# Constant-operand matmuls in the filler bank where a planned kernel leaves TensorE without work

## The chip, the cores and the metric

The program runs on one core of a Trainium2 chip. The metric is the device time of one execution in microseconds (us). The engines' names are those of the profile: PE is TensorE's matmul side and PEld its weight loads, ACT is ScalarE, DVE is VectorE, POOL is GpSimd, SP is SyncE, whose queue issues most DMAs.

## The reference

Four layers run one after the other over an activation `x` of 2048 tokens by 1024 features, each with a residual: A, B, A, B. Both kinds have 32 heads of 32 features. Kind A is linear attention with softmax feature maps, kind B is full softmax attention without a mask:

```python
def _A_ref(x, wqkv, w_phi, wo):
    ...
    phi_q = jnp.concatenate([_softmax(pq, axis=-1), _softmax(-pq, axis=-1)], axis=-1)
    phi_k = jnp.concatenate([_softmax(pk, axis=-1), _softmax(-pk, axis=-1)], axis=-1)
    kv = jnp.einsum("bhsf,bhsd->bhfd", phi_k, v)
    ...
def _B_ref(x, wqkv, wo):
    ...
    scores = jnp.einsum("bhqd,bhkd->bhqk", q, k) * (Dh ** -0.5)
    p = _softmax(scores, axis=-1)
    o = jnp.einsum("bhqk,bhkd->bhqd", p, v)
    ...
x = x + _A_ref(_layernorm(x, axis=-1), A_wqkv, A_w_phi, A_wo)
x = x + _B_ref(_layernorm(x, axis=-1), B_wqkv, B_wo)
x = x + _A_ref(_layernorm(x, axis=-1), A_wqkv, A_w_phi, A_wo)
x = x + _B_ref(_layernorm(x, axis=-1), B_wqkv, B_wo)
```

In each B layer 32 heads x 2048 x 2048 scores, 134 million, go through an exponential.

## The kernel before, in words

The activation lives in SBUF transposed, in `xT`: 8 slabs of 128 features by 2048 tokens. The tokens are worked on in four chunks of 512. The program is written as a list of operations (`Op`: an engine, a modelled duration, what it depends on, the buffers that it holds and a priority). `Sched.run` is a planner in Python that plays this list through once, before anything is built: each modelled engine takes, when it is free, the ready operation of lowest priority number whose buffers can be had. The order that comes out is the order in which the instructions are then written, so on the chip every engine follows a fixed list. The planner's clock is a model and never changes speed (`MM` = 0.2165 us for a 512-column matmul).

PSUM has eight banks of 512 columns. In a B layer's attention they are shared out: banks 0 to 2 and 3 to 5 are two score buffers (class `S`), bank 6 collects one output (class `acc`), and bank 7 is the filler bank (`FIL`, class `fil`).

Attention goes in steps, which are called steps here throughout. A step covers three units; a unit is one head, one chunk of 512 queries and one block of 128 keys. In a step:
- three score matmuls of 32 rows each fill three banks (line 886, in `attention`); they lie beside each other in TensorE's rows;
- one ACTIVATE takes the exponential of all three banks, 128 x 1536 (line 892). A later step may write those banks once it is done;
- six matmuls of 32 columns each add V and the sum of the exponentials to bank 6 (line 920). They are issued four together, beside each other in TensorE's columns.

A B layer has 4096 units, so 1366 steps in both. Query chunks 0 and 1 are done first, head group by head group, then chunk 2 and then chunk 3 for all groups.

All other matmuls that fall into attention are fillers: the keys, values and queries of later head groups (`b_k`, `b_v`, `b_q`, `q_away`), the output projections of finished query chunks (`b_o`, in the last layer `b_last`, line 847), and in the first B layer the next A layer's keys. Each filler is a group of eight matmuls of 128 x 512 in four operations, accumulating in bank 7, which is held from the group's first matmul until its result has been read out. Fillers take the bank strictly in the order of their priorities. A projection group needs the eight head groups' outputs `oT[0]` to `oT[7]`, and each of its four operations waits for two of them alone.

The names that matter below: line 886 is the score matmul, line 892 the exponential, line 920 the V and sum matmul, line 847 a filler of the last projection, `onesD` a constant 128 x 128 matrix, `Sched.live` the count of buffers in use by class, `bank_used` the state of the eight banks.

Of the kernel before, what the change touches and what calls it, by code (L numbers as in the profile page):

```python
# [18 lines left out]
C512 = 512  # L19
# [3 lines left out]
class Buf:  # L23
# [4 lines left out]
    def __init__(self, kind, size, cls, banks=None):  # L28
        self.kind, self.size, self.cls, self.banks = kind, size, cls, banks
        self.left, self.at, self.with_ = 0, None, ()  # L30
# [11 lines left out]
LAT = {"PE": 0.25, "ACT": 0.2, "DVE": 0.1, "POOL": 0.2, "SP": 2.0, "AQ": 2.0}  # L42
# [3 lines left out]
class Sched:  # L46
    def __init__(self, sbuf_bytes, quota):
        self.ops = []
        self.quota = quota
        self.live = {}  # L50
        self.free = [(0, sbuf_bytes)]
        self.bank_used = [False] * 8
        self.peak = 0
        self.total = sbuf_bytes
        self.queue = {}

    def op(self, eng, dur, fn, deps=(), bufs=(), prio=0.0, lat=None, mode=None):
        o = Op(eng, dur, LAT[eng] if lat is None else lat, fn, tuple(bufs), prio, mode, len(self.ops))
        for d in deps:
            if d is not None:  # L60
                d.out.append(o)
                o.ndep += 1
        for b in o.bufs:
            b.left += 1
        self.ops.append(o)
        return o
# [75 lines left out]
    def run(self):  # L142
        engines = list(LAT)
        ready = {e: [] for e in engines}
        busy = {e: 0.0 for e in engines}
        mode = {e: None for e in engines}
        events = []
        n = 0

        first = {}  # L150
        for o in self.ops:
            for b in o.bufs:
                k = (o.prio, o.seq)
                for x in (b, *b.with_):
                    if id(x) not in first or k < first[id(x)][0]:
                        first[id(x)] = (k, x)
        for k, b in sorted(first.values(), key=lambda f: f[0]):
            self.queue.setdefault(b.cls, [[], 0])[0].append(b)
        todo = sorted(o.prio for o in self.ops)
        front = 0  # L160
        started = {}
        for o in self.ops:
            if o.ndep == 0:
                heapq.heappush(ready[o.eng], (o.prio, o.seq, o))
        t, left, order = 0.0, len(self.ops), []
        while left:
            moved = False
            for e in engines:
                if busy[e] > t + 1e-9 or not ready[e]:
                    continue  # L170
                skipped = []
                pick = None
                while ready[e] and len(skipped) < 60:
                    item = heapq.heappop(ready[e])
                    if item[0] <= todo[front] + WINDOW and self._alloc(item[2].bufs):
                        pick = item[2]
                        break
                    skipped.append(item)
                for s in skipped:
                    heapq.heappush(ready[e], s)  # L180
                if pick is None:
                    continue
                d = pick.dur
                if pick.mode is not None:
                    if mode[e] is not None and mode[e] != pick.mode:
                        d += SWITCH
                    mode[e] = pick.mode
                pick.start = t
                started[pick.prio] = started.get(pick.prio, 0) + 1
                while front < len(todo) - 1 and started.get(todo[front], 0):  # L190
                    started[todo[front]] -= 1
                    front += 1
                busy[e] = t + d
                order.append(pick)
                left -= 1
                moved = True
                n += 1
                heapq.heappush(events, (t + d, n, pick, True))
                n += 1
                heapq.heappush(events, (t + d + pick.lat, n, pick, False))  # L200
            if moved:
                continue
            if not events:
                stuck = [(o.prio, o.eng, [(b.cls, b.at) for b in o.bufs]) for e in engines for _, _, o in ready[e]][:8]
                raise AssertionError(f"nothing can start at {t:.1f}: {left} left, {stuck}, live {self.live}")
            t = events[0][0]
            while events and events[0][0] <= t + 1e-9:
                _, _, o, own = heapq.heappop(events)
                if not own:
                    for b in o.bufs:  # L210
                        b.left -= 1
                        if b.left == 0:
                            self._release(b)
                for x in o.out:

                    if own != (x.eng == o.eng and x.eng not in ("SP", "AQ")):
                        continue
                    x.ndep -= 1
                    if x.ndep == 0:
                        heapq.heappush(ready[x.eng], (x.prio, x.seq, x))  # L220
        self.end = t
        return order
# [8 lines left out]
         "e": 6, "vp": 6, "e1": 4, "vp1": 4, "E": 5, "q2": 3, "kt": 3, "w2": 8, "w2o": 3, "oT": 26, "T": 4, "den": 2,  # L231
         "lnt": 6, "lnw": 2, "lnw1": 1, "eq": 8, "ns": 4, "cw": 6, "hl": 6, "oc": 2, "slab": 7, "slabk": 3, "fin": 4,
         "rs": 8, "pkf": 1}


def act_us(n):
# [7 lines left out]
MM = 0.2165  # L244
# [3 lines left out]
def kernel(  # L248
# [11 lines left out]
    nc = tc.nc  # L260
    P = nc.NUM_PARTITIONS
    _, S, D = A_x.shape
    PO = D // P
    G = PO
# [20 lines left out]
    onesD = const.tile([P, P], BF16, tag="onesD")  # L285
# [6 lines left out]
    pick = const.tile([P, 4], F32, tag="pick")  # L292
# [30 lines left out]
    xT = const.tile([P, PO, S], BF16, tag="xT")  # L323
    ARENA = SBUF_ARENA
    arena = arena_p.tile([P, ARENA // 2], BF16, tag="arena")
    psum = psum_p.tile([P, 8 * C512], F32, tag="psum")
# [10 lines left out]
    sch = Sched(ARENA, QUOTA)  # L337
# [31 lines left out]
    TAIL = [(x,) for x in (7, 0, 1, 2, 3, 4, 5)]  # L369
# [96 lines left out]
    def slab(cls, prio, src, n, deps=(), q="SP"):  # L466
        b, v = sb(cls, PO, n)
        o = dma(prio, lambda: (nc.sync if q == "SP" else nc.scalar).dma_start(out=v(), in_=src),
                deps, [b], q=q, kb=2 * n)
        return b, v, [o] * 4  # L470
# [352 lines left out]
    def b_o(ft, c, prio, w, oT, banks, after=None):  # L823
        wb, ww, wd = w
        pb, pv = ps("fil", banks)
        m = mmg2(pb, pv, lambda po: ww()[:, po, :], lambda po: oT[po][1](),
                 [[oT[2 * i][2], oT[2 * i + 1][2], after] for i in range(4)], wd,
                 [wb] + [oT[i][0] for i in range(G)], prio)
        return op("DVE", dve_us(512), lambda: nc.vector.tensor_tensor(
            out=xT[:, ft, csl(c)], in0=xT[:, ft, csl(c)], in1=pv(), op=ALU.add), [m], [pb], prio)  # L830
# [148 lines left out]
    for layer in range(2):  # L979
# [73 lines left out]
        oTs, last_s = attention(at, kT, vT, q_of, gate)  # L1053
        if last:
            bo_s = [slab("slab", at + 160 + fc, B_o[:, :, fc * C512:(fc + 1) * C512], C512) for fc in range(2)]
        for qc, p0, gap, banks in ((0, 163, 1.5, FIL), (1, 176, 1.5, FIL), (2, 251, 1.5, FIL), (3, 340, 1, TAIL)):
            after = last_s if banks is TAIL else None
            if last:
                gap = {0: 6, 1: 6, 2: 9, 3: 1}[qc]
                p0 = {0: 163, 1: 200, 2: 251, 3: 340}[qc]  # L1060
                for t in range(TB):
                    for fc in range(2):
                        b_last(qc, t, fc, at + p0 + gap * (2 * t + fc), bo_s[fc], oTs[qc], banks,
                               ("ACT", "DVE")[fc] if banks is TAIL else "DVE", after)
            else:
                adds = []
                for ft in range(G):
                    w = slab("w2o", at + p0 + gap * ft - 6, B_o[:, :, ft * P:(ft + 1) * P], P)
                    adds.append(b_o(ft, qc, at + p0 + gap * ft, w, oTs[qc], banks, after))
                xdone[qc] = adds  # L1070
        if not last:

            kv = new_kv()
            for c, p0 in ((0, 190), (1, 220), (2, 265)):
                xb, xv, fin = xnA[c] = layernorm(c, at + p0, FIL, True)
                w = [(wk_slab(at + p0 + 2 + 14 * fc, fc, "slabk"), wv_slab(at + p0 + 2.5 + 14 * fc, fc, cls="slabk")) for fc in range(2)]
                a_keys(c, at + p0 + 2, [w[0][0], w[1][0]], [w[0][1], w[1][1]], kv, FIL, True, 3.5)
                xnA[c] = dma(at + p0 + 4, lambda c=c, xv=xv: nc.sync.dma_start(
                    out=xd_v[:, c, :, :], in_=xv()), fin, [xb], kb=1024)

    for o in sch.run():
        o.fn()
# [30 lines left out]
```

## Time and profile before

| what | value |
| --- | --- |
| median of 3 runs | 2716.61 us (2715.13 to 2718.79) |
| the profiled execution's own time | 2719.31 us |
| its span, first to last instruction | 2717.5 us |
| PE busy | 2417.6 us (89%) |
| ACT busy | 2194.0 us (81%) |
| DVE busy | 1136.0 us (42%) |
| mean granted TensorE clock | 0.906 |

Busy time of PE is read with care: its matmuls overlap, and a matmul takes twice as long when the granted clock is 0.50 (1.2 GHz) as when it is 1.00 (2.4 GHz). A busy PE at half clock does half the work. A window's clock between the two is the mean of stretches at either level.

### The profile page before, as it was taken

The numbers are of one execution on the slowest core, as the hardware profiler recorded it, in microseconds if no ns is written. First come the engines' busy times: TensorE is split into PE (matmuls) and PEld (weight loads), VectorE is DVE, ScalarE is ACT, GpSimd is POOL, SyncE is SP. The second block draws the span as 40 slices with busy tenths as digits, with TensorE's granted clock in tenths as the row PEclk, the third lists the DMA queues.
The fourth block names the chain that finished last, engine by engine and source line by source line (L and its number), as shares of the span: only waits on it lengthen the run. The fifth ranks groups of instructions, "written<-read, shape, count | busy, mean of one in ns | idle before, by whom it ended". The sixth has DMA issues, their size and how long they took to land.

```text
span 2717.5 us, 42396 instructions
## 1 busy us (share of the span) xinstructions
PE 2417.6 (89%) x17730; PEld 774.3 (28%) x17984; DVE 1136.0 (42%) x1614; ACT 2194.0 (81%) x1919; POOL 25.3 (1%) x72
## 2 busy tenths in 40 slices
PE   5999998999988988989888999999998898888887
PEld 2443332222222222332313333222222122112112
DVE  4996653333322335655516665233333222222112
ACT  5335546999999999999983553899999999999995
POOL 0000000000000000000000000000000000000000
PEclk9999999999997889999969999999998698668657
DMA  7120003111121212224122000311211011001000
GB/s 166 42 65 1 5 4 65 42 32 45 37 57 40 56 39 65 78 71 119 30 64 97 1 6 3 74 36 34 67 34 26 18 38 32 18 16 32 19 12 22
DMA packets 185760, 116.08 MB, mean 43 GB/s; under 512 B 103904, under 2 KB 175584, under 8 KB 184800
## 3 DMA queue, kind: packets, MB, share of 16 engines
q1 hardware_dynamic: 181344, 109.10, 15.3%
q10 hardware_dynamic: 4224, 4.26, 0.6%
q8 instruction: 140, 2.29, 0.4%
q14 instruction: 52, 0.43, 0.1%
HBM read 61.93 MB, written 15.73 MB: 29 GB/s over the span
## 4 chain that ended last, share of the span: by engine, by line
ACT 45%; PE 35%; issue 10%; DVE 7%; DMA 2%; SPq 1%; ACTq 0%; DVEq 0%
ACT arena L892 43%; PE psum L619 16%; PE psum L920 8%; PE psum L886 5%; DVE arena L562 2%; SPq L404 1%; PE psum L714 1%; DVE arena L571 1%; PE psum L383 1%; DVE arena L460 1%; PE psum L847 1%; ACT arena L558 1%; DVE arena L456 1%; DVE arena L608 1%; PE psum L701 1%
## 5 line engine op out<-in xcount | busy, mean ns | idle before, releaser
L892 ACT ACTIVATE arena<-psum 128x1536 bf16<-128x1536 f32 (+1 forms) x1366 | 1859.8, 1505 | 92.8 <-PE psum L886 50.6
L619 PE MATMUL psum<-arena 128*128 128x512 bf16 x3631 | 954.1, 386 | 60.1 <-DVE arena L460 19.9
L920 PE MATMUL psum<-arena 128*32 128x512 bf16 x4096 | 800.7, 436 | 16.1 <-ACT arena L892 10.2
L920 PE MATMUL psum<-arena,ones_bf 128*32 128x512 bf16 x4096 | 801.6, 437 | 0.0
L886 PE MATMUL psum<-arena 32*128 32x512 bf16 x4096 | 590.0, 428 | 162.6 <-ACT arena L892 152.2
L619 PEld LDWEIGHTS <-arena 128*128 128x128 bf16 x3840 | 318.7, 98 | 562.7 <-issue 282.2
L886 PEld LDWEIGHTS <-arena 32*128 32x128 bf16 x4096 | 167.0, 92 | 708.2 <-issue 698.5
L932 DVE COPY arena<-psum 128x512 f32<-128x512 f32 x128 | 88.4, 691 | 599.7 <-PE psum L920 597.3
L920 PEld LDWEIGHTS <-arena 128*32 128x32 bf16 x4096 | 160.5, 96 | 396.8 <-issue 391.0
L943 DVE RECIPROCAL arena<-arena 128x128 f32<-128x128 f32 x256 | 219.1, 912 | 77.3 <-DMA arena<-arena 76.0
L778 DVE CAST arena<-psum 128x512 bf16<-128x512 f32 x116 | 80.1, 690 | 333.4 <-PE psum L619 211.1
L920 PEld LDWEIGHTS <-ones_bf 128*32 128x32 bf16 x4096 | 158.3, 96 | 47.6 <-issue 46.9
L423 ACT ACTIVATE arena<-xT 128x2048 bf16<-128x2048 bf16 x26 | 50.1, 1934 | 105.4 <-DVE xT L754 40.5
L558 ACT ACTIVATE arena<-psum 128x512 bf16<-128x512 f32 x80 | 43.2, 610 | 101.3 <-PE psum L619 68.6
L671 ACT ACTIVATE arena<-psum 128x512 bf16<-128x512 f32 x128 | 70.3, 598 | 43.6 <-PE psum L619 39.2
L456 DVE TENSOR_TENSOR arena<-xT,arena 128x1024 f32<-128x1024 bf16 x64 | 78.0, 1220 | 63.9 <-ACT arena L445 63.4
L947 DVE TENSOR_TENSOR arena<-arena 64x512 bf16<-64x512 f32 x128 | 87.8, 686 | 29.1 <-PE psum L920 20.8
L777 ACT CAST arena<-psum 128x512 bf16<-128x512 f32 x44 | 25.5, 584 | 88.0 <-PE psum L619 66.8
L571 DVE TENSOR_TENSOR arena<-psum,arena 128x1024 bf16<-128x1024 f32 x64 | 78.3, 1224 | 42.8 <-PE psum L619 38.7
L460 DVE TENSOR_TENSOR arena<-arena 128x1024 bf16<-128x1024 f32 x64 | 77.2, 1224 | 21.3 <-ACT arena L450 20.0
L562 DVE TENSOR_REDUCE arena<-arena 128x32 f32<-128x1024 bf16 x64 | 77.7, 1213 | 16.6 <-ACT arena L558 15.5
L718 ACT COPY arena<-psum 128x512 f32<-128x512 f32 x64 | 37.3, 583 | 55.4 <-PE psum L714 46.6
(79 smaller groups left out, 955.2 us busy)
## 6 DMA issues: line engine op xcount, KB each, us to landing
arena<-arena SPq DMA_DIRECT2D x128, 128.0 KB, 2.3
arena<-in_B_wqkv_dram SPq DMA_DIRECT2D x32, 256.0 KB, 4.6
arena<-arena SPq DMA_DIRECT2D x256, 32.0 KB, 1.9
arena<-in_B_wo_dram SPq DMA_DIRECT2D x32, 256.0 KB, 3.2
arena<-wd_k SPq DMA_DIRECT2D x8, 1024.0 KB, 5.8
arena<-in_A_wqkv_dram SPq DMA_DIRECT2D x8, 1024.0 KB, 5.3
arena<-in_A_wqkv_dram ACTq DMA_DIRECT2D x4, 1024.0 KB, 6.1
arena<-in_A_wo_dram SPq DMA_DIRECT2D x4, 1024.0 KB, 7.2
```

Of the source, the lines that this page charges most:

```text
L456: s1 = op("DVE", dve_us(1024), lambda pr=pr, w_v=w_v: nc.vector.tensor_tensor(out=w_v(), in0=xT[:, pr, csl(c)], in1=m_v().unsqueeze(1).to_ ...
L460: fin.append(op("DVE", dve_us(1024), lambda pr=pr, w_v=w_v: nc.vector.tensor_tensor(out=xv()[:, pr, :], in0=w_v(), in1=r_v().unsqueeze(1). ...
L562: red = op("DVE", dve_us(1024), lambda ev=ev, sv=sv: nc.vector.reduce_sum(out=sv(), in_=ev().rearrange("p s (h d) -> p (s h) d", d=DH), ax ...
L571: ml = op("DVE", dve_us(1024), lambda vpv=vpv, wv_=wv_, sv=sv: nc.vector.tensor_tensor(out=wv_()[:, :, :, 0:DH], in0=vpv().rearrange("p (h ...
L619: nc.tensor.matmul(pv(), lhsT=lhs(po), rhs=rhs(po), start=(po == 0), stop=(po == PO - 1))
L778: return op("DVE", dve_us(512), lambda: nc.vector.tensor_copy(out=dst(), in_=src()), [dep], bufs, prio)
L886: nc.tensor.matmul(out=s_v()[:, x * C512:(x + 1) * C512], lhsT=kT[g][1]()[r, pp, d * P:(d + 1) * P], rhs=q_of[(qc, g)][1]()[r, (pp + j // ...
L892: ex = op("ACT", act_us(w * C512), lambda s_v=s_v, e_v=e_v, w=w: nc.scalar.activation(out=e_v()[:, 0:w * C512], in_=s_v(), func=ACT.Exp), ...
L920: nc.tensor.matmul(out=a_v()[col:col + 32, :], lhsT=v_v()[:, kc % 4, o:o + DH] if what == 0 else ones_bf[:], rhs=ev()[:, x * C512:(x + 1) ...
L932: cp = op("DVE", dve_us(512), lambda t_v=t_v, a_v=a_v: nc.vector.tensor_copy(out=t_v(), in_=a_v()), [last], [a_b, t_b], prio - 4)
L943: rc = [op("DVE", 128 * 8 / 960 + 0.12, lambda b=b, d_v=d_v, r_v=r_v: nc.vector.reciprocal(out=r_v()[:, b * P:(b + 1) * P], in_=d_v()[:, b ...
L947: s = [op("DVE", dve_us(512), lambda a=a, b=b, k=k, o_v=o_v, r_v=r_v, T=T: nc.vector.tensor_tensor(out=o_v()[a, :], in0=T[k][1]()[a, :], i ...
```

## The change

Three things are added. The planner gets an operation `idle`: one 128 x 512 matmul of `onesD` by the first chunk of `xT`, written to bank 7, whose result nobody reads. When the modelled TensorE is free, nothing that is ready can start, a score buffer is live, the modelled TensorE has worked less than 75% (`KEEP`) of the last 3.4 us (`SPELL`), no filler is live and bank 7 is free, an `idle` is placed. Last, the projections of chunks 0 to 2 wait with their first matmul until the last head group's output is there; before, they had no such wait.

```diff
+                if pick is None and e == "PE" and self.idle is not None and self.live.get("S", 0):
+
+                    recent = [r for r in recent if r[1] > t - SPELL]
+                    worked = sum(r[1] - max(r[0], t - SPELL) for r in recent)
+                    if worked < KEEP * SPELL and not self.live.get("fil", 0) and not self.bank_used[7]:
+                        pick = Op("PE", MM, LAT["PE"], self.idle, (Buf("ps", 0, "idle", [(7,)]),), 0.0, "n", 0)
+                        pick.bufs[0].left = 1
+                        self.queue["idle"] = [list(pick.bufs), 0]
+                        assert self._alloc(pick.bufs)
+                        left += 1
                 if pick is None:
                     continue
+                if e == "PE":
+                    recent.append((t, t + pick.dur))
...
-                started[pick.prio] = started.get(pick.prio, 0) + 1
+                if pick.fn is not self.idle:
+                    started[pick.prio] = started.get(pick.prio, 0) + 1
...
+SPELL = 3.4
+KEEP = 0.75
...
-            after = last_s if banks is TAIL else None
+            after = [last_s] if banks is TAIL else oTs[qc][G - 1][2]
...
+    def idle():
+        nc.tensor.matmul(psum[:, 7 * C512:8 * C512], lhsT=onesD[:], rhs=xT[:, 0, 0:C512], start=True, stop=True)
+    sch.idle = idle
```

The built program has 562 such matmuls, line 1099, each with a weight load. Counted from the order by steps (0 to 682 in the first B layer, 683 to 1365 in the second): 63 in steps 287 to 328, 20 in 405 to 416, 7 in 573 to 576, 62 in 641 to 681, 5 at the second layer's start, 63 in 970 to 1011, 159 in 1098 to 1203, 176 in 1247 to 1364, and 7 alone. In steps 264 to 277 and 947 to 960 there is neither a filler nor an `idle`. Other lines of the kernel move by 17: line 886 becomes 903, line 920 becomes 937, line 847 becomes 864.

First place: PE late in the second B layer's attention, just ahead of the scores of step 1262, before. `arena` and `psum` are the work areas in SBUF and PSUM, and a wait on Activation is a wait for ScalarE.

```order
L920 LDWEIGHTS arena
L920 MATMUL psum<-arena 32x512
L920 LDWEIGHTS ones_bf
L920 MATMUL psum<-arena,ones_bf 32x512
L886 LDWEIGHTS arena
L886 MATMUL psum<-arena 128x512 [waits Activation_49]
```

The same place on PE now:

```order
L937 LDWEIGHTS arena
L937 MATMUL psum<-arena 32x512
L937 LDWEIGHTS ones_bf
L937 MATMUL psum<-arena,ones_bf 32x512
L1099 LDWEIGHTS onesD
L1099 MATMUL psum<-xT,onesD 128x512
L903 LDWEIGHTS arena
L903 MATMUL psum<-arena 128x512 [waits Activation_49]
```

Between the V and sum matmuls and the next scores, which wait for an exponential, there is now one `idle`, which waits for nothing.

Second place: PE in the second B layer, just ahead of the scores of step 1120, before. Line 847 is an operation of the projection of query chunk 2.

```order
L920 LDWEIGHTS ones_bf
L920 MATMUL psum<-arena,ones_bf 32x512
L847 LDWEIGHTS arena
L847 MATMUL psum<-arena 128x512
L847 LDWEIGHTS arena [waits DVE_49]
L847 MATMUL psum<-arena 128x512
L886 LDWEIGHTS arena
L886 MATMUL psum<-arena 128x512 [waits Activation_49]
```

The same place on PE now:

```order
L937 LDWEIGHTS ones_bf
L937 MATMUL psum<-arena,ones_bf 32x512
L1099 LDWEIGHTS onesD
L1099 MATMUL psum<-xT,onesD 128x512
L903 LDWEIGHTS arena
L903 MATMUL psum<-arena 128x512 [waits Activation_49]
```

Before, the group's eight matmuls stood two by two in steps 1089, 1119, 1162 and 1204, and held bank 7 all that while; now they stand together in steps 1204 to 1207, and steps 1098 to 1203 hold `idle` matmuls.

## Rows read from the trace of the kernel before

**Rows 1.** The page: busy tenths in 40 slices, and the granted clock.

```profile
PE   5999998999988988989888999999998898888887
ACT  5335546999999999999983553899999999999995
PEclk9999999999997889999969999999998698668657
```

**Rows 2.** Waits: engine, line and what it waited for; total us, times, longest.

```profile
PE psum L886 <- ACT arena L892: 152.2, 326, 1.5
...
ACT arena L892 <- PE psum L886: 50.6, 59, 2.3
...
ACT arena L892 <- PE psum L920: 38.3, 95, 0.5
```

**Rows 3.** Line 892 alone by stretch: length, ACT busy and count, clock, DMA.

```profile
1944.50:2078.90 134.40, 134.28 (x100) 1.00 0.18 48
904.80:920.40 15.60, 15.60 (x12) 1.00 0.32 77
448.30:499.60 51.30, 48.40 (x37) 1.00 0.17 41
831.10:892.70 61.60, 57.35 (x42) 0.68 0.09 22
998.40:1017.40 19.00, 16.16 (x12) 0.68 0.07 18
1360.60:1420.30 59.70, 55.98 (x41) 0.65 0.25 71
2109.70:2172.00 62.30, 57.73 (x42) 0.66 0.08 20
2290.00:2449.40 159.40, 146.25 (x106) 0.63 0.07 17
2509.10:2688.20 179.10, 163.09 (x118) 0.60 0.05 13
2597.60:2658.80 61.20, 54.67 (x40) 0.50 0.03 7
...
2082.00:2100.00 18.00, 15.19 (x11) 0.53 0.05 13
```

**Rows 4.** All engines by stretch: PE, PEld, DVE, ACT, POOL busy (count), clock.

```profile
1944.50:2078.90 134.40, 125.23 (x1066) 35.18 (x1084) 45.24 (x61) 134.28 (x100) 0.00 (x0) 1.00 0.18 48
920.70:936.90 16.20, 14.25 (x126) 4.16 (x128) 6.40 (x8) 16.10 (x14) 0.00 (x0) 1.00 0.38 89
2290.00:2449.40 159.40, 130.76 (x956) 29.82 (x956) 30.72 (x40) 146.25 (x106) 0.00 (x0) 0.63 0.07 17
2597.60:2658.80 61.20, 53.59 (x353) 11.05 (x350) 9.46 (x14) 54.67 (x40) 0.00 (x0) 0.50 0.03 7
998.40:1017.40 19.00, 13.84 (x112) 3.46 (x109) 9.28 (x11) 17.30 (x14) 0.00 (x0) 0.68 0.07 18
```

**Rows 5.** PE in order of time, half clock, no filler: start, length, what.

```profile
2625.95 0.61 PE L886 MATMUL psum<-arena 32*128 32x512 bf16 x3 [0.64 <-ACT arena L892]
...
2627.46 0.61 PE L886 MATMUL psum<-arena 32*128 32x512 bf16 x3
...
2629.15 0.61 PE L886 MATMUL psum<-arena 32*128 32x512 bf16 x3 [0.53 <-ACT arena L892]
```

**Rows 6.** ACT in order of time, the same stretch.

```profile
2627.64 2.79 ACT L892 ACTIVATE arena<-psum 128x1536 bf16<-128x1536 f32 x2 [0.41 <-PE psum L920]
2630.84 2.79 ACT L892 ACTIVATE arena<-psum 128x1536 bf16<-128x1536 f32 x2 [0.41 <-PE psum L920]
```

**Rows 7.** PE in order of time, full clock, no filler.

```profile
2517.67 0.40 PE L886 MATMUL psum<-arena 32*128 32x512 bf16 x3 [0.62 <-ACT arena L892]
...
2519.02 0.39 PE L886 MATMUL psum<-arena 32*128 32x512 bf16 x3 [0.41 <-ACT arena L892]
...
2520.36 0.39 PE L886 MATMUL psum<-arena 32*128 32x512 bf16 x3 [0.62 <-ACT arena L892]
```

**Rows 8.** PE in order of time, full clock, with fillers of line 847.

```profile
2467.72 0.39 PE L886 MATMUL psum<-arena 32*128 32x512 bf16 x3
2468.04 1.04 PE L847 MATMUL psum<-arena 128*128 128x512 bf16 x4
2469.01 0.39 PE L920 MATMUL psum<-arena 128*32 128x512 bf16 x1
...
2469.66 0.61 PE L847 MATMUL psum<-arena 128*128 128x512 bf16 x2
2470.20 0.39 PE L886 MATMUL psum<-arena 32*128 32x512 bf16 x3
```

**Rows 9.** PE in order of time, half clock at the end, line 847.

```profile
2688.22 1.49 PE L847 MATMUL psum<-arena 128*128 128x512 bf16 x3 [0.33 <-issue]
...
2689.63 0.39 PE L920 MATMUL psum<-arena 128*32 128x512 bf16 x1
```

More of the change, by code (lines that the diff above doesn't have):

```diff
@@ L55, in __init__ @@
         self.queue = {}
+        self.idle = None
     def op(self, eng, dur, fn, deps=(), bufs=(), prio=0.0, lat=None, mode=None):
@@ L160, in run @@
         front = 0
+        recent = []
         started = {}
```

## The prediction

> **What bounds the kernel now.** I read the slices of the page first, since they set the stages apart [rows 1]. Through both B layers' attentions (slices 7 to 20 and 26 to 39) ACT is at 9 tenths or more except at the layer's edge, and PE is at 8 or 9 beside it. Their sums say little on which of the two holds the other up. The clock row does: it stands at 9 until the fillers become rare and falls to 5 to 8 in the last third of each attention.
>
> So I went to stretches of the exponential's line alone [rows 3]. Between 1944 and 2079 us, at clock 1.00, 100 exponentials take 134.4 us and ACT is busy for 134.28 of it: ACT is the bound, with nothing left. Every window of rows 3 is cut to begin 0.3 us (the one at 1360.6: 0.6 us) after its first exponential, so that the one before is not counted; I add this back everywhere. The pace at full clock is then 134.7 / 100 = 1.347 us a step. Between 2597.6 and 2658.8 the clock is 0.50, 40 exponentials take 61.5 us, 1.54 us each, and ACT is busy for 54.67 alone. What differs between the two is PE's list [rows 4]: a step has 9 matmuls, so 1066 in 100 steps are 166 fillers, 1.66 a step, and 353 in 40 steps (360 expected, some records are missing) are none.
>
> The order in time shows how the half clock gets into the end. At half clock two steps take 2625.95 to 2629.15, 3.20 us, and PE stands still for no more than 0.53 to 0.64 us in them [rows 5]; in each pair ACT waits 0.41 us for the V and sum matmuls [rows 6]. At full clock without fillers the pair takes 2517.67 to 2520.36, 2.69 us, and PE is idle for 0.62 and 0.41 of it [rows 7]. So an attention step without fillers leaves PE idle, its clock drops, and then PE is what ACT waits for. All that ACT waits on line 886 and line 920 is 50.6 + 38.3 = 88.9 us over the run [rows 2]: no change to PE's clock in attention can bring much more than that.
>
> **Part 1: the 562 idle matmuls.** By the counts in the section on the change, 543 of them lie in six stretches of 361 steps: 1.50 a step, where before there were 14 fillers in all. The nearest rows on what this does to the clock are those at 1.66 fillers a step, clock 1.00 for 134 us, and a short one at 920.7, where 126 matmuls in 12 steps make 18 fillers, 1.50 a step, and the clock is also 1.00 [rows 4]. At none a step it is 0.50 for 61 us, and 0.63 over the stretch 2290 to 2449, whose 956 matmuls in 106 steps are two more than nothing. I take full clock in the six stretches. What that is worth, with both paces in time from exponential to exponential [rows 3]:
> - 831 to 893: 61.9 - 42 x 1.347 = 5.3 us
> - 998 to 1017: 19.3 - 12 x 1.347 = 3.1, of which 17.30 - 16.16 = 1.1 us are other work of ACT that stays [rows 4]: 2.0 us
> - 1360 to 1420: 60.3 - 41 x 1.347 = 5.1 us
> - 2109 to 2172: 62.6 - 42 x 1.347 = 6.0 us
> - 2290 to 2449: 159.7 - 106 x 1.347 = 16.9 us
> - 2509 to 2688: 179.4 - 118 x 1.347 = 20.5 us
>
> The sum is 55.8 us. The 19 others lie where the clock is mostly full; I give them nothing.
>
> What the idle matmuls cost: at full clock two fillers between one step's scores and the next take 2469.66 to 2470.20, 0.54 us [rows 8]; one takes 0.54 less one matmul. A matmul is worth (2469.01 - 2468.04 - 0.54) / 2 = 0.215 us by the four and the two of them in rows 8, so one costs 0.32 us with the change of tile shape. Three in two steps are 0.86 us, and PE is idle for 0.62 + 0.41 = 1.03 us in them [rows 7]. They fit, with 0.17 us over, and what hides them is the exponential of the other score buffer, which runs for 1.3 us meanwhile. The first place in the order shows where one stands: ahead of score matmuls that wait for an exponential anyway. If that cover is too short, the scores come late by up to 0.54 us, and ACT stands only by what this exceeds PE's slack. Bounds for the pace: 15.9 / 12 = 1.33 us at best, the fastest full-clock stretch, and 51.3 / 37 = 1.39 at worst, the stretch at 448 with its many fillers [rows 3]. Over 361 steps that is 6 us more or 16 us less than 55.8. I take 1.347, the row with the nearest number of fillers.
>
> Eleven idle matmuls wait, on DVE or ACT, for the reader of bank 7 or a write of `xT`; all others follow in PE's list with no wait. Nothing else is put past a queue: ACT's order changes in about ten places, by a step or two, DVE's and SP's in about twenty; what moves there is fillers' work, and ACT, the bound of these stretches, waits for none of it.
>
> **Part 2: the projections wait for the last head group.** The second place in the order shows what moves: six matmuls of a group that stood in steps 1089, 1119 and 1162 now stand with the last two in steps 1204 to 1207. Six at 0.215 are 1.3 us later for this group, and the next filler takes the bank about three steps later; what lies behind are projections that are due long before the attention ends, and ACT does not wait for them. I give it nothing. Without this wait bank 7 would be held there and the 159 idle matmuls of that stretch could not have been placed, so the 16.9 us hang on it.
>
> **What stays.** In steps 264 to 277 and 947 to 960 no idle matmul is placed. The second is at 0.53 now [rows 3] and loses 18.0 - 11 x 1.347 = 3.2 us there; I leave that in. The end after 2688 stays, but for three projections at half clock that take 2688.22 to 2689.63 [rows 9] and could win 1.41 - 0.65 = 0.8 us. The profiled execution took 2719.3 us, 2.7 more than the median of the runs: 2719.3 - 56 = 2663, and against the median 2716.6 - 56 = 2660.
>
> **A rule against it.** In rows 5 and 7 PE never stands for more than 0.64 us, and the longest of its 326 waits for an exponential is 1.5 us [rows 2], yet the clock falls to 0.50. The Trainium skill, page TensorE: Matmul & The Clock Gate, section HAM oscillation, puts a fall of the clock down to TensorE standing idle for longer than any of these gaps. By that alone, filling gaps of half a microsecond would win none of the 56 us; this is the condition of rival C. Its next section, A second HAM failure mode, names another case, small idle times between groups of matmuls, and with that one the trace agrees.
>
> **The rivals.**
> A. The clock holds but the idle matmuls are in the way of the scores, and the pace is nearer 1.39. For it: every filler-rich stretch is slower than 1.347. Against it: these fillers also bring work for DVE and other engines, and idle matmuls bring none. It gives 55.8 - 16 = 40 us, 2677.
> B. The clock holds only in part: the planner's clock knows no half speed, so on the chip the matmuls may bunch where they are not needed. With half of the steps won, 28 us: 2689.
> C. The slower side: the half clock has another cause than PE's idle time and stays as it is. Then each idle matmul is work on the engine that is the bound. At half clock one costs 1.41 / 3 = 0.47 us [rows 9]; three in a pair of steps are 1.41 us, of which 0.53 fall into idle time [rows 5], so a step takes 1.60 + 0.44 = 2.04. The six stretches are at half clock for about 74% of their time now (mean clock 0.63), and 361 x 0.74 x 0.44 = 118 us more: 2835. It decides once more than 0.22 of these steps stay at half clock, since 1.347 + 0.22 x (2.04 - 1.347) = 1.50, the mean of the six now (543.2 us less the 1.1, over 361). Against it: the clock and the fillers go together in every row that I have, and a PE with that much to do at half clock has no idle time left.
> D. It does not do what it says: the idle matmuls find PE's gaps, but ACT gains nothing, since its wait turns to something else, as DVE's reading of bank 6. Then 2717. Against it: at full clock with fillers ACT is idle for 0.1 us in 134 [rows 3].
>
> **How the numbers follow.** Forecast 70%, 2660 us, with its own range 2648 (pace 1.33, and the bare steps of the last layer and their like in the first also won) to 2670. A 13%, B 8%, C 5%, D 4%. From these, 2643 to 2690 holds the forecast, A and most of B's centre. Within 0.2%, 5.4 us, is about what cannot be told from no change: D and a little of B and C, 4%. Faster 91%, slower 5%.
>
> **What the profile after would show.** Right: the clock slices of the last third of both attentions at 9, with steps 264 to 277 and 947 to 960 as the only dips; line 892 at about 1.35 us a step in the six stretches and its waits on lines 903 and 937 down from 88.9 to some 30 us; line 1099 at 562 matmuls, most after a step without idle time behind it on ACT. Wrong: line 892 waiting for line 903 at full clock (A), stretches at half clock with idle matmuls in them and steps of 2 us (C), or full clock with an unchanged pace (D).

## The result and the profile after

The changed kernel takes 2657.18 us (median of 4 runs, 2654.41 to 2658.36), the kernel before 2717.31 beside it. The ratio is 0.9774, 95% interval 0.9762 to 0.9786. Forecast were 2660 us, 2643 to 2690. The profiled execution took 2658.36 us, its span is 2656.5.

The slices of the page after, against [rows 1]:

```profile
PE   4999998999998999899998999899999899999998
ACT  4334545999989999999994455599999999999996
PEclk9999998999998999999999999999999999999999
```

The clock no longer falls in the last third of either attention. Its mean went from 0.906 to 0.984. The exponential (now line 909) alone, in the same six stretches of steps as in [rows 3], again from 0.3 us behind the first exponential's start (a B layer has 2048 units, which are 683 steps; the 4096 units and 1366 steps are those of both B layers together):

```profile
839.31:895.30 55.99, 55.99 (x42) 1.00 0.08 20
998.21:1015.82 17.61, 16.13 (x12) 1.00 0.09 23
1354.82:1409.57 54.75, 54.75 (x42) 1.00 0.27 78
2095.43:2151.39 55.96, 55.96 (x42) 1.00 0.08 20
2267.50:2409.45 141.95, 141.95 (x106) 1.00 0.08 20
2469.05:2627.03 157.98, 157.98 (x118) 1.00 0.06 15
```

In five of them ACT is busy for the whole window (the 42 of the third are 41 and the end of one before; in the second, ACT does other work beside). One line of ACT in order of time says it best: 75 exponentials with no gap.

```profile
2499.60 101.00 ACT L909 ACTIVATE arena<-psum 128x1536 bf16<-128x1536 f32 x75
```

PE in order of time in that stretch; line 903 are the scores, line 1099 the idle matmuls, and the V and sum matmuls between them (line 937) are left out:

```profile
2542.09 0.39 PE L903 MATMUL psum<-arena 32*128 32x512 bf16 x3
2542.41 0.39 PE L1099 MATMUL psum<-xT,onesD 128*128 128x512 bf16 x1
...
2543.22 0.39 PE L903 MATMUL psum<-arena 32*128 32x512 bf16 x3
2543.55 0.60 PE L1099 MATMUL psum<-xT,onesD 128*128 128x512 bf16 x2
2544.23 0.39 PE L903 MATMUL psum<-arena 32*128 32x512 bf16 x3
```

These scores carry no wait for an exponential as those in [rows 5, 7] do; idle matmuls stand in its place. The waits, against [rows 2]:

```profile
PE psum L903 <- ACT arena L909: 57.9, 148, 1.1
...
ACT arena L909 <- PE psum L903: 43.4, 41, 3.4
...
ACT arena L909 <- PE psum L937: 2.9, 7, 0.4
```

What ACT waits on the V and sum matmuls is gone (38.3 to 2.9 us), what it waits on the scores has hardly changed (50.6 to 43.4).

### The profile page after: what moved, and what is told of

It reads as the page before. It is cut to its first block, busy times and chain, and to the rows that moved or that the text cites. A ratio compares the mean times of both kernels' runs of the same rounds, so it can differ in the third digit from the quotient of the medians.

```text
span 2656.5 us, 43877 instructions
## 1 busy us (share of the span) xinstructions
PE 2462.1 (93%) x18546; PEld 818.9 (31%) x18546; DVE 1135.4 (43%) x1614; ACT 2179.4 (82%) x1919; POOL 25.7 (1%) x72
## 4 chain that ended last, share of the span: by engine, by line
ACT 46%; PE 31%; issue 11%; DVE 8%; DMA 2%; SPq 1%; ACTq 0%; DVEq 0%
ACT arena L909 44%; PE psum L636 18%; PE psum L937 5%; PE psum L903 3%; DVE arena L579 2%; DVE arena L477 1%; SPq L421 1%; DVE arena L473 1%; PE psum L731 1%; PE psum L400 1%; DVE arena L588 1%; PE psum L864 1%; ACT arena L575 1%; DVE arena L625 1%; DMA arena<-arena 1%
## 5 line engine op out<-in xcount | busy, mean ns | idle before, releaser
L909 ACT ACTIVATE arena<-psum 128x1536 bf16<-128x1536 f32 (+1 forms) x1366 | 1845.6, 1562 | 47.5 <-PE psum L903 43.4
L636 PE MATMUL psum<-arena 128*128 128x512 bf16 x3840 | 987.3, 385 | 41.3 <-DVE arena L477 15.8
L937 PE MATMUL psum<-arena 128*32 128x512 bf16 x4096 | 705.6, 390 | 10.2 <-ACT arena L909 6.7
L937 PE MATMUL psum<-arena,ones_bf 128*32 128x512 bf16 x4096 | 706.8, 390 | 0.0
L903 PE MATMUL psum<-arena 32*128 32x512 bf16 x4096 | 534.2, 386 | 84.7 <-ACT arena L909 57.9
L903 PEld LDWEIGHTS <-arena 32*128 32x128 bf16 x4096 | 174.8, 91 | 553.7 <-issue 527.0
L1099 PE MATMUL psum<-xT,onesD 128*128 128x512 bf16 x562 | 188.0, 386 | 0.3
```

The lines of the kernel that those rows point to most:

```text
L636: nc.tensor.matmul(pv(), lhsT=lhs(po), rhs=rhs(po), start=(po == 0), stop=(po == PO - 1))
L903: nc.tensor.matmul(out=s_v()[:, x * C512:(x + 1) * C512], lhsT=kT[g][1]()[r, pp, d * P:(d + 1) * P], rhs=q_of[(qc, g)][1]()[r, (pp + j // ...
L909: ex = op("ACT", act_us(w * C512), lambda s_v=s_v, e_v=e_v, w=w: nc.scalar.activation(out=e_v()[:, 0:w * C512], in_=s_v(), func=ACT.Exp), ...
L937: nc.tensor.matmul(out=a_v()[col:col + 32, :], lhsT=v_v()[:, kc % 4, o:o + DH] if what == 0 else ones_bf[:], rhs=ev()[:, x * C512:(x + 1) ...
L1099: nc.tensor.matmul(psum[:, 7 * C512:8 * C512], lhsT=onesD[:], rhs=xT[:, 0, 0:C512], start=True, stop=True)
```

## The experiments

Two theories stood at first. K: the idle matmuls hold PE's clock at full, and that is all of it. O: the wait of the projections and the new order do it. A third, E, came from the third run. In the table "clock" is the mean granted clock of steps 1098 to 1203 and 1247 to 1364, which hold 335 of the 543 idle matmuls; us are those of the two together, 339.1 before and 300.6 in the changed kernel. Each ratio is to runs of the kernel before on the same chip, whose medians were 2717 to 2723 us.

| run | median us | ratio to before, interval | us in the two stretches | clock in each |
| --- | --- | --- | --- | --- |
| before | 2717.3 | | 339.1 | 0.63, 0.60 |
| changed | 2657.2 | 0.9774 (0.9762 to 0.9786) | 300.6 | 1.00, 1.00 |
| e1 wait alone | 2726.5 | 1.0024 (1.0012 to 1.0037) | 341.7 | 0.58, 0.57 |
| e2 idle alone | 2687.9 | 0.9876 (0.9854 to 0.9898) | 320.1 | 0.60, 1.00 |
| e3 narrow | 2710.6 | 0.9962 (0.9950 to 0.9974) | 331.9 | 0.53, 0.51 |
| e4, 178 of them | 2658.8 | 0.9774 (0.9758 to 0.9789) | 302.0 | 1.00, 0.97 |
| e5 rotated, before | 2666.0 | 0.9787 (0.9772 to 0.9802) | 305.7 | 0.71, 0.70 |
| e6 doubled | 2715.9 | 0.9978 (0.9965 to 0.9991) | 339.2 | 1.00, 1.00 |
| e8 rotated, changed | 2649.1 | 0.9735 (0.9718 to 0.9751) | 300.6 | 1.00, 1.00 |
| e9 rotated, doubled | 2712.2 | 0.9963 (0.9949 to 0.9977) | 338.6 | 1.00, 1.00 |

**e1, the wait without idle matmuls.**

```diff
-    sch.idle = idle
+    sch.idle = None
```

> The projections wait for the last head group as in the changed kernel, but no idle matmul is placed. Theory K (the clock: the time went because the idle matmuls keep PE's clock at full): as the kernel before, 2717 us within 5, the clock 0.6 to 0.7 in steps 287 to 328, 970 to 1011, 1098 to 1203 and 1247 to 1364. Theory O (the order: the wait frees bank 7 and lets the list of work run closer): most of the 60 us is kept, under 2690 us.

Measured: 2726.5 us, 0.24% slower than before. The two stretches by line 909:

```profile
2296.77:2458.51 161.74, 146.74 (x107) 0.58 0.07 18
2517.86:2697.19 179.33, 163.24 (x118) 0.57 0.05 13
```

O falls. The wait alone costs a little: the four projection matmuls that stood in the first of the two are gone, its clock is 0.58 for 0.63, and it takes 162.1 us for 159.7.

**e2, idle matmuls without the wait.**

```diff
-            after = [last_s] if banks is TAIL else oTs[qc][G - 1][2]
+            after = [last_s] if banks is TAIL else None
```

> Idle matmuls as in the changed kernel, but the projections of chunks 0 to 2 start with their first matmul at once, as before. 323 idle matmuls are placed by the order: 29 in steps 287 to 306, 26 in 401 to 416, 62 in 641 to 681, 187 in 1240 to 1364, and none in 307 to 328, 970 to 1011 and 1098 to 1203. Theory K: the stretches without them fall back to half clock and lose what they had won (6.3 and 17.4 us, and half of 5.7): 2657 + 26 = 2683 us, the others keep it. Theory O: no gain left, near 2717. If the wait has no part in it: 2657.

Measured: 2687.9 us. The stretch that lost its idle matmuls, and the one that kept them, by line 909:

```profile
2277.71:2439.06 161.35, 146.65 (x106) 0.60 0.07 17
2498.74:2656.82 158.08, 158.08 (x118) 1.00 0.06 15
```

One fell back to the time of before, the other holds at 1.00. So the wait is worth some 30 us, but only by freeing bank 7 for idle matmuls.

**e3, narrow idle matmuls.**

```diff
-        nc.tensor.matmul(psum[:, 7 * C512:8 * C512], lhsT=onesD[:], rhs=xT[:, 0, 0:C512], start=True, stop=True)
+        nc.tensor.matmul(psum[:, 7 * C512:7 * C512 + 32], lhsT=onesD[:], rhs=xT[:, 0, 0:32], start=True, stop=True)
```

> The same list of instructions as the changed kernel, 562 idle matmuls in the same places, but each has 32 columns instead of 512. Theory K, with the work of PE as what holds the clock: the half clock comes back in all six stretches and the time goes to 2717 us, or a few us above by the change of tile shape. Rival N (any instruction of full shape in the gap is enough): stays at 2657 us.

Measured: 2710.6 us. The half clock is back, even more of it, and with it the time, so an instruction in the gap is not enough. But 8 us are missing, and the rows were odd:

```profile
2285.46:2441.64 156.18, 147.56 (x106) 0.53 0.07 18
2502.21:2677.24 175.03, 164.66 (x118) 0.51 0.06 14
```

At a lower clock than before the steps are faster. ACT in order of time shows nine exponentials with no gap at half clock, where in [rows 6] two at a time are followed by 0.41 us of waiting:

```profile
2586.96 12.93 ACT L909 ACTIVATE arena<-psum 128x1536 bf16<-128x1536 f32 x9 [0.41 <-PE psum L937]
```

Its waits on the V and sum matmuls are 9.7 us in all, against 38.3. So the half clock alone does not make ACT wait for them. The nine still take 1.44 us each, against 1.347 at full clock: here PE has the narrow matmuls in its list as well, and it waits for no more than 0.2 us in all. What a step takes at half clock without them is seen in e5.

**e4, fewer idle matmuls.**

```diff
-KEEP = 0.75
+KEEP = 0.45
```

> KEEP is 0.45 instead of 0.75: 178 idle matmuls in the same six stretches, 0.48 a step instead of 1.50. If the gain goes with their number: 57 x 178 / 562 = 18 us, 2699 us. Theory K with a level at which the clock holds, under this number: the clock stays full in most of the stretches, 2657 to 2670 us; with the level above it: half clock in most of them, 2700 us or more, and the idle matmuls are then work at half clock.

Measured: 2658.8 us, the changed kernel's time with a third of the idle matmuls. The gain does not go with their number.

```profile
2265.27:2407.22 141.95, 141.95 (x106) 1.00 0.08 19
2466.78:2626.15 159.37, 158.66 (x118) 0.97 0.06 15
```

**e5, theory E.** What does the exponential wait for when it waits for V and sum matmuls? For the SBUF buffer that it writes: they read the exponentials of an earlier step from it. The planner gives out the free space at the highest address, which is as a rule the buffer freed last (in 184 of the 224 steps of the two stretches, by its plan); the shortest times in the plan, from the start of the last read to the next write, are 0.48 us. The kernel before was given a choice of the buffer freed longest ago, nothing else (`olds` holds freed addresses, oldest first). The order that the planner writes stays the same but for 12 of PE's 6030 operations and 3 of ACT's 1918:

```diff
+                old = self.olds if b.cls == "E" and len(self.olds) >= SPARE else ()
+                for x in old:
+                    i = next((i for i, (lo, n) in enumerate(self.free) if lo <= x and x + b.size <= lo + n), None)
+                    if i is not None:
...
+                        b.at = x
+                        break
...
+            if b.cls == "E":
+                self.olds = [x for x in self.olds if abs(x - b.at) >= b.size] + [b.at]
+SPARE = 2
```

> The kernel before, without idle matmuls and without the wait; alone the planner's choice of the SBUF buffer that an exponential writes is changed: it takes the one that was freed longest ago, not the one at the highest address. In the plan the shortest times from the last read of such a buffer to the next exponential into it go from 0.5 us to over 2.8 (tenth percentile). Theory E (at half clock ACT waits for the V and sum matmuls because they still read the buffer that it is to write): the 38 us of waits of the exponential on the V and sum matmuls go, half clock stays, 2690 to 2705 us. If these waits only turn into waits for the scores: 2717 us.

Measured: 2666.0 us, more than theory E had expected: with no idle matmul and no wait, 57 of the 60 us (beside it the kernel before took 2723.1). The two stretches, and a window of it at half clock throughout, by the exponential's line:

```profile
2268.95:2413.40 144.45, 142.91 (x107) 0.71 0.07 19
2472.47:2633.06 160.59, 159.16 (x118) 0.70 0.06 15
```

```profile
2594.00:2606.00 12.00, 11.76 (x9) 0.50 0.01 2
```

At a mean clock of 0.70 a step takes 160.9 / 118 = 1.36 us, against 1.52 before, and at half clock itself ACT is busy for 11.76 of 12 us. PE in that window (the scores; the V and sum matmuls between them are left out):

```profile
2596.58 0.61 PE L904 MATMUL psum<-arena 32*128 32x512 bf16 x3
...
2597.75 0.61 PE L904 MATMUL psum<-arena 32*128 32x512 bf16 x3
...
2599.27 0.61 PE L904 MATMUL psum<-arena 32*128 32x512 bf16 x3
```

Two steps of PE's list take 2.69 us at half clock and wait for nothing, 1.345 us a step. In steps 287 to 328, 970 to 1011, 1098 to 1203 and 1247 to 1364, those steps that lie at half clock from start to end take 1.37 us each here (146 of them), 1.57 in the kernel before (196) and 1.48 in e3 (274); at full clock it is 1.34 here and before.

The waits of the exponential on PE in this run are the scores' alone; there is no row for the V and sum matmuls any more:

```profile
ACT arena L910 <- PE psum L904: 45.8, 54, 2.1
```

**e6, doubled idle matmuls.**

```diff
     def idle():
-        nc.tensor.matmul(psum[:, 7 * C512:8 * C512], lhsT=onesD[:], rhs=xT[:, 0, 0:C512], start=True, stop=True)
+        for _ in range(2):
+            nc.tensor.matmul(psum[:, 7 * C512:8 * C512], lhsT=onesD[:], rhs=xT[:, 0, 0:C512], start=True, stop=True)
```

> The changed kernel with two matmuls in place of each idle matmul, 1124. By the sum of the prediction three idle matmuls fit into two steps with 0.17 us over; six take 6 x 0.215 + 0.2 = 1.5 us against 1.03 us of idle time, 0.47 us too much in two steps, so the six stretches go at 1.58 us a step: 361 x 0.235 = 85 us more, 2742 us. If the idle matmuls are hidden with more room than that sum says (the scores need not follow at once): 2657 to 2670 us.

Measured: 2715.9 us. All of the gain is gone at full clock: 178.4 / 118 = 1.51 us a step. All engines by stretch (columns as in rows 4):

```profile
2504.94:2683.06 178.12, 178.12 (x1412) 48.81 (x1411) 31.41 (x41) 165.04 (x118) 0.00 (x0) 1.00 0.06 14
```

PE is busy from end to end. A pair of steps takes 3.02 us; the prediction's sum gives 3.16.

**e9, doubled and rotated.** Both edits together.

> Two matmuls for each idle matmul, as in the doubled kernel, and the exponential's buffer taken by the longest time free, as in the rotated ones. Theory E (the doubled kernel is slow at full clock because the V and sum matmuls, pushed back by 0.2 us for each added matmul, hold the buffer that the next exponential is to write): that wait goes, the six stretches are at 1.35 us a step again, 2650 to 2660 us. Theory P (PE's work as such is the bound: 0.47 us too much in two steps): as the doubled kernel, 2716 us, or 2735 by the prediction's own sum.

Measured: 2712.2 us. Theory E had this wrong: with rotated buffers the waits move to the scores (69.7 us in all, none on the V and sum matmuls), and the time stays. With that much work PE itself is the bound.

```profile
2503.25:2681.12 177.87, 174.65 (x1386) 48.72 (x1409) 31.40 (x41) 165.98 (x118) 0.00 (x0) 1.00 0.06 14
```

**e8, the changed kernel with rotated buffers.**

> The changed kernel with the same choice of the exponential's buffer as in the kernel before with rotated buffers. Theory E: it matters at half clock alone, of which 87 us are left, most of them outside attention: 2654 to 2657 us, at most 3 us under the changed kernel.

Measured: 2649.1 us, the fastest of all; its interval lies wholly under the changed kernel's. The order is the changed kernel's on every engine, operation for operation; only addresses differ. The six stretches are the same to 0.1 us. In the profiles, 2.8 of the 9.2 us between the spans lie in steps 100 to 263, 2.1 in steps 264 to 286 and 947 to 969, which have no idle matmuls, and the rest in pieces of about 1 us. It is more than the 3 us expected at most. Part of that expectation was wrong: of the 87 us at half clock that the changed kernel has left, 48 lie in attention. And the 2.8 us are not shown to come from the buffers: every kernel here has the same order in steps 100 to 263, on every engine, and the profiled executions spread from 225.9 to 233.4 us there.

**e7, e10, e11, e12, a fourth query buffer.** In steps 264 to 277 and 947 to 960 bank 7 is held by a query's result that waits for one of three buffers. With four (`"q2": 4`) the fillers behind it move up to steps 266 to 272 and 949 to 955, and idle matmuls stand in 273 to 286 and 956 to 969.

> The changed kernel with four query buffers instead of three, so that a query's result need not stay in bank 7 until an older query is used up. In the plan, idle matmuls then stand in steps 273 to 286 and 956 to 969 too (616 in all), which are at 0.8 clock now and cost about 1.4 us a place over 1.347 us a step; in the second layer fillers are spread anew. Theory K: these two dips go, 2654 us, 2 to 3 us under the changed kernel; no change if the dips are hidden.

> The changed kernel with rotated exponential buffers and four query buffers together. If the two add up: the rotated kernel's 2649 us less 2 to 3 us for the two places without idle matmuls, 2646 us; if these places cost nothing any more once the buffers rotate: 2649 us.

> As the last, and idle matmuls are also placed where no score buffer is live: 35 more, 19 ahead of the first attention and 16 between it and the second. The half clock left there is some 30 us at 410 to 440, 1416 to 1426 and 1680 to 1688 us; where PE is the bound in them, a few us are to be won: 2643 us. If PE waits for others there: no change, 2646 us.

> Rotated exponential buffers, four query buffers, and KEEP at 0.45: 187 idle matmuls instead of 616. By the run with 178, fewer are enough: 2646 us, as with 616, within 2 us.

Measured: e7 2655.3 us (0.9755, 0.9739 to 0.9772), which cannot be told from the changed kernel. Its steps 264 to 286 and 947 to 969 are at 1.00 and take 61.8 us for 66.3, as K has it, but steps 417 to 572 take 243.3 for 235.2: the fillers there, the next layer's keys, are spread anew, and ACT waits more. e10 2656.9 (0.9761, 0.9747 to 0.9774), e11 2654.9 (0.9755, 0.9742 to 0.9768) and e12 2654.4 (0.9752, 0.9739 to 0.9766): the medians of these three, with rotated buffers, are 5 to 8 us over e8's, though their intervals still touch e8's, and steps 417 to 572 are again the place (242.7, 242.9 and 241.7 us for 235.3). e10 has e7's order on every engine, so with four query buffers the rotation wins nothing that these runs can tell. The two edits don't add up; 35 more idle matmuls or 429 fewer make no difference that these runs can tell.

## Why the prediction was right, and where not

**The sum.** By stretch, forecast and measured: 5.3 and 5.7, 2.0 and 1.4, 5.1 and 5.3, 6.0 and 6.3, 16.9 and 17.4, 20.5 and 21.1 us; 55.8 and 57.2 together. The pace is 158.3 / 118 = 1.342 us for the 1.347 taken. Full clock in the six stretches, the cover for the idle matmuls, the part of the wait in bank 7 (e2), the nothing for the 19 others and the bare steps that stay (32.9 us for 34.4 in steps 947 to 969) all came as said. (The upper bound of the pace left out the 0.3 us that is added elsewhere: 51.6 / 37 is 1.395, not 1.386, which changes nothing.) The spans differ by 61.0 us, so 3.8 come from elsewhere, in both directions: steps 329 to 404 and 417 to 572 win 6.0, steps 100 to 263 lose 6.8. The loss is not shown to be the change's: the order there is the same before and after, and 233.4 us is the top of the spread named at e8. Part of it is a wait of 3.6 us, of a filler for DVE's reading of bank 7 (1.1 at most before), which itself waits 8.4 us for a store to leave its buffer (5.8 before):

```profile
DVE arena L795 <- DMA qd<-arena: 8.4, 1, 8.4
...
PE psum L636 <- DVE arena L795: 3.6, 1, 3.6
```

**The step that was wrong is in the reading of the bound**: "its clock drops, and then PE is what ACT waits for". At half clock PE's list is just short enough for ACT: 1.345 us a step in e5, where ACT's pace at full clock is 1.347. [rows 5] had it: of 3.20 us for two steps PE stands still for 0.53, which leaves 2.67 of work. What made it late was a second condition, which [rows 6] had shown without my asking why: the exponential waited for the matmuls that still read the buffer it was to write, because the planner as a rule gave out the buffer freed last. Either condition taken away gives nearly all of the time back: full clock (the change, e4) or another buffer (e5). The forecast could not tell them apart, since the change takes away the first and its sum uses paces that were measured at either clock; so the number came out right although this step was wrong. It also means that the ceiling drawn from [rows 2] was right in size and wrong in name.

**The cost of the idle matmuls.** Three in two steps were to fit with 0.17 us over. e6 shows three more to cost 3.02 - 2.68 = 0.34 us for a pair, where the sum gives 0.47; the room is about 0.3 us. It is real and small: twice the number eats the whole gain (e6, e9). e4 shows that a third of it would have done.

**The waits after** were to be 30 us and are 46.3. In the last four stretches none is left; nearly half of the rest, 22.3 us, lies between 420 and 800 us, where fillers are dense and the change does nothing. I had counted too little of the 88.9 to such places.

**The rule against it.** In e1 PE's longest wait for an exponential in the two stretches is 1.0 us, and the clock is at half for about 85% of the time; with 0.48 idle matmuls a step in e4 it is full for nearly all. So the clock fell with no gap longer than that. The Trainium skill, page TensorE: Matmul & The Clock Gate, section A second HAM failure mode, tells of a clock that falls with small idle times between groups of matmuls, and e1 agrees with it, not with the one idle gap of its section HAM oscillation. Gaps alone do not decide it: in e4 PE still waits for an exponential 83 times in 106 steps, up to 0.6 us, and the clock is 1.00; in e3, with an instruction in the same places as in the changed kernel, it is 0.53. Rival C needed another cause for the half clock, which stays whatever fills the gaps; the changed kernel's 1.00 beside e1's 0.58 and 0.57 excludes it. A, B and D did not come: the pace held, the clock held, and ACT turned to nothing else. The two places without idle matmuls are not the only dips, as the prediction had it: five shorter ones in attention make up half of the 48 us.

What is left open: why e8 wins 9 us over the changed kernel where theory E had 3 at most, while e10 wins none over e7; and how far e3's 8 us are due to its buffers alone, since its list differs from e1's in the idle matmuls too.

## What to carry to other kernels

An engine at half clock need not cost much (1.37 us a step in e5 for 1.34 at full clock): ask which wait its lateness ends in, and whether a buffer given out in another order takes that wait away, before work is added to lift the clock. A free list that hands out the buffer freed last ties the writer to the latest reader; the one freed longest ago cost nothing here. Where idle matmuls are placed, try how few hold the clock, since their room is small and at twice the number PE was the bound.

## What was not expected of the hardware

Idle matmuls at 0.48 a step, 51 weight loads above the plain list in 106 steps, held the clock at 1.00 for 142 us (e4); at none a step it stood at 0.50 for 61 us [rows 3]. With 562 matmuls of 32 columns in the same places it was 0.51 to 0.53 (e3), lower than with none (0.57 and 0.58 in e1): their number alone did nothing for it.
